# Pooled attention and a squared-ReLU feed-forward: scores as cross products on all rows and the main product on row halves, with a new planned order

## The chip, the cores and the metric

One Trainium2 chip, one core. Times are device microseconds of the whole kernel; the median of three runs before the change is 878.62 us.

## What is computed

```python
def _attn_ref(q, k, v):                       # q, k, v: (4, 8, 1152, 64), float32
    q_pool = q.reshape(B, H, S // 2, 2, D).mean(axis=3)
    scores = (1.0 / np.sqrt(D)) * np.matmul(q_pool, k.transpose(0, 1, 3, 2))
    scores = scores - np.max(scores, axis=-1, keepdims=True)
    attn = np.exp(scores)
    attn = attn / (np.sum(attn, axis=-1, keepdims=True) + 1e-09)
    return np.matmul(attn, v).astype(np.float32)

def _moe_ref(x, w_in, w_out):                 # x: (2304, 512), w_in: (512, 2048), w_out: (2048, 512)
    h = x @ w_in
    r = np.maximum(h, 0.0)
    return ((r * r) @ w_out).astype(np.float32)
```

`reference` puts the heads of `_attn_ref` side by side, 8 x 64 = 512 columns for 4 x 576 rows, and hands them to `_moe_ref`. The feed-forward part works on all rows with one pair of weights.

## The kernel before

Every float32 operand of a product is carried as two float16 parts, a high one (hi) and what is left (lo), and a product is a sum of products of parts in float32. The work falls into **heads in pairs**: 4 batches by 4 pairs are 16 preparations; each pair has nine chunks of 128 queries, 144 chunks in all. Eight of the nine belong to one head (128 queries); the fifth in the list `CH` (its entry is `None`) holds the last 64 queries of both heads. I call the first kind a full and the second a narrow unit.

*Preparation of a pair* (`prep`). k, q and v are loaded (`LK`, `LQ`, `LV`, on the SyncE queue), q is pooled (`QS`), a scale is found, and the parts are written: `KA` writes the hi part of k (a scaled copy, line 315 or 317, on ScalarE or GpSimd), `KD` the lo part (VectorE, line 343, one instruction a head), `KT` transposes both by DMA into a tile `kT` (line 488): its partitions 0 to 63 are the hi part, 64 to 127 the lo part, and its columns the keys in blocks of 128, nine a head. `QA`, `QD`, `QT` do the same for q into `qT[:, 0]`. `QX` (line 509, VectorE or GpSimd) copies the two partition halves of `qT[:, 0]` into `qT[:, 1]` swapped, so that there the lo part is on top. `VA` and `VD` split v.

*A chunk* (`chunk`). `S` makes the scores: for l = 0 (hi on hi plus lo on lo) and l = 1 (lo on hi plus hi on lo) and three stretches of keys (512, 512, 128), a product of all 128 rows into one of two tiles `s` of three PSUM banks (line 572; line 567 for narrow units, whose two heads use one half of the output columns each). `MX` takes the row maximum (VectorE, line 580), `EX` the exponential with its row sum (ScalarE, lines 590 and 591) into a buffer. Then the result is split and transposed: for most chunks `HI` (ScalarE line 595, GpSimd line 340, or VectorE line 599), `LO` (line 603, VectorE or GpSimd) and a DMA transpose `TR` into `PT`; for 28 chunks TensorE transposes (`TP`, line 658) with `TH` and `TL` (lines 667 and 681) copying out. `S` of chunk i waits for `EX` of chunk i - 2.

*A group* (`group`). `PV` (line 723) multiplies the transposed weights with v, two heads at a time on the two halves of the output columns: 54 products of 256 or 320 columns. `ED` copies out.

*Feed-forward blocks* (`block`). Nine blocks of 256 rows: normalise (`RV` to `XR`), scale and split (`XQ` to `XD`), `H` in 8 steps of 24 products of 256 columns (line 865), ReLU and square (`HA` line 875 or 877, `G1` 880, `G2` 885 or 888, `G3` 892), `O` in 8 steps of 12 products of 512 columns (line 914), `OD` and the store. The weights of this part are prepared while attention runs (`WL` to `WD`).

*Order.* Nothing is ordered by hand. `Plan.add` takes each step with its engines and a duration for each in ns, and `Plan.order` builds a list: among the steps that could start soonest, the one with the smallest `prio` goes first, which is its place in the program plus an offset for its kind from `CFG` (`off`, and `off0` before chunk `FB`, behind which the first block could begin). Where a step may run on several engines, the planner picks. The list is issued as it stands: each engine works through its instructions in this order.

Of the kernel before, what the change touches and what calls it, by code (L numbers as in the profile page):

```python
# [56 lines left out]
class Plan:  # L57
# [15 lines left out]
    def add(self, name, engs, deps, emit, at, take=None, give=None, after=()):  # L73

        kind = name[0]
        off, off0 = cfg("off", {}), cfg("off0", {})
        self.at[name] = len(self.ops)
        prio = cfg("nudge", {}).get(len(self.ops), 0.0) + at + off.get(kind, DEF.get(kind, 0.0)) + (off0.get(kind, 0.0) if at < self.early else 0.0)
        self.ops.append(
            dict(name=name, engs=dict(engs), deps=[d for d in deps if d], emit=emit, pos=at, prio=prio, take=take, give=give, after=after)  # L80
        )

    def order(self, last):
# [127 lines left out]
def kernel(  # L211
# [12 lines left out]
    nc = tc.nc  # L224
    B, H, S, D = q.shape
# [7 lines left out]
    KD = DM // 128  # L233
# [63 lines left out]
    add = plan.add  # L297
    tl = {}
# [14 lines left out]
    def scaled(o, out, x, s):  # L313
        if o["eng"] == "ACT":
            nc.scalar.activation(out, x, AF.Copy, scale=s)
        elif o["eng"] == "POOL":
            nc.gpsimd.tensor_scalar(out, x, s, 1.0, op0=ALU.mult, op1=ALU.mult)  # L317
        else:
            nc.vector.tensor_scalar(out, x, s, None, op0=ALU.mult)
# [26 lines left out]
    def prep(n):  # L346
# [39 lines left out]
        def k2():  # L386
            return buf("k2", n).rearrange("p (h c l d) -> p h c l d", h=2, c=9, l=2)
# [89 lines left out]
            add(("GE", n, w), {"POOL": 350}, [("GU", n, w)], lambda o, w=w: ge(o, w), need)  # L477

        def ka(o):
            scaled(o, k2()[:, :, :, 0, :], rk(), tl["psc", n][:, 2, 0:1])  # L480

        def kd(o):
            t, r, s = k2(), rk(), tl["psc", n][:, 2, 0:1]
            for h in range(2):
                split_lo(t[:, h, :, 1, :], r[:, h], s, t[:, h, :, 0, :])

        def kt(o):
            nc.sync.dma_start_transpose(out=kTs[slot], in_=buf("k2", n))
# [51 lines left out]
    def chunk(i):  # L540
# [15 lines left out]
        def scores(o):  # L556
            s = sts[i % 2]
            kt, qt = kTs[slot], qTs[slot]
            for l in range(2):
                for x in range(3):  # L560
                    for h in range(2) if CH[j] is None else CH[j][:1]:
                        st = dict(start=(l == 0), stop=(l == 1), skip_group_check=True)
                        k0, k1 = 4 * x, min(4 * x + 4, 9)
                        rhs = kt[:, h * 9 + k0 : h * 9 + k1, :].rearrange("p a b -> p (a b)")
                        w = 128 * (k1 - k0)
                        if CH[j] is None:
                            nc.tensor.matmul(
                                s[h * 64 : (h + 1) * 64, x, :w], lhsT=qt[:, l, h, 8, :], rhs=rhs, **st
                            )
                        else:  # L570
                            c0 = CH[j][1]
                            nc.tensor.matmul(  # L572
                                s[:, x, :w], lhsT=qt[:, l, h, c0 : c0 + 2, :].rearrange("p a b -> p (a b)"),
                                rhs=rhs, **st
                            )

        def smax(o):
            a = sm_p.tile([128, 2], F32, tag="ca", name="ca", bufs=4)
# [40 lines left out]
        back = []  # L619
        if i >= 2:  # L620
            back = [("TL", i - 2)] if i - 2 in turned and i - 2 not in turned_b else [("EX", i - 2)]
        add(("S", i), {"PE": 1115 if CH[j] is None else 985}, [("KT", n), ("QX", n)] + back, scores, i)
        add(("MX", i), {"DVE": 1275}, [("S", i)], smax, i)
        add(("EX", i), {"ACT": 1500}, [("MX", i), ("GE", n, "qk")] + sold, ex, i, take=(("P", i), ("buf",), cfg("RSV", 1)))

# [77 lines left out]


    GR_ = [0, 1, 1, 0]

    def group(vi, r):
        n, js, i0 = visits[vi]
# [6 lines left out]
        def pv(o):  # L715
            vv = v2s[preps[n]["slot"]]
            px = bank(o)
            tl["px", vi, r] = px
            ps = [(vl, pl, kc) for vl, pl in ((1, 0), (0, 0), (0, 1)) for kc in range(NC)]
            for i, (vl, pl, kc) in enumerate(ps):  # L720
                for h in range(2):
                    t = PTs[gidx[vi, gg[h]] % NPT]
                    nc.tensor.matmul(  # L723
                        px[h * 64 : (h + 1) * 64, :N], lhsT=vv[:, h, kc, vl, :], rhs=t[:, 9 * pl + kc, :N],
                        start=(i == 0), stop=(i == 3 * NC - 1), skip_group_check=True,
                    )

# [466 lines left out]
```

## Time and profile before

| | before |
|---|---|
| median of 3 runs | 878.62 us (876.68 to 881.27) |
| span of the profiled execution | 873.5 us |
| median of the runs less that span | 5.1 us |
| TensorE busy | 743.7 us (85%), 6041 products |
| VectorE busy | 653.3 us (75%) |
| ScalarE busy | 610.7 us (70%) |
| GpSimd busy | 403.0 us (46%) |
| mean granted TensorE clock | 0.946 |

No time of its own is listed for the profiled execution beside its span; the 5.1 us is what the runs' median has above it. Busy times are unions of an engine's instructions, and the ends of products are modelled: what a group of products takes is read from the start of one group to the start of the next, where nothing waits between them. The granted clock is 1.00 at 2.4 GHz and 0.5 at 1.2 GHz; a mean between them is a mix of both. Line numbers are those of the kernel before.

### The profile page before, as it was taken

What the parts mean: (1) busy time and instruction counts of PE and PEld (TensorE: products, weight loads), DVE (VectorE), ACT (ScalarE), POOL (GpSimd) and SP (SyncE); (2) the same over time, 40 slices, a digit from 0 to 9 for tenths busy, and PEclk for the clock granted to TensorE, in tenths of its full rate; (3) what the DMA queues carried; (4) which work ended last, traced back from release to release, by engine and by line L of the source; (5) the groups of instructions that cost most, each with busy time, mean ns of one, the idle gap of its engine ahead of it and who ended that gap; (6) DMA issues with size and microseconds to landing.
All of it is one profiled execution on the core that took longest, in us unless ns stands there. A gap on an engine that the chain in (4) does not pass through costs nothing. (4 is left out here: it accounts for less than half of the span.)

```text
span 873.5 us, 15476 instructions
## 1 busy us (share of the span) xinstructions
PE 743.7 (85%) x6041; PEld 495.6 (57%) x6041; DVE 653.3 (75%) x817; ACT 610.7 (70%) x959; POOL 403.0 (46%) x281
## 2 busy tenths in 40 slices
PE   0567656767579999998999999898999999999997
PEld 0344534544347567754775576566647756858573
DVE  4897999997878887988989788879788974312120
ACT  4666886778988778866896767777767984625150
POOL 2454436755878644555465266537835531100000
PEclk9976877799869999999999999999999999999999
DMA  7798796797668999989998989996889997000001
GB/s 220 223 176 210 163 245 179 184 220 150 134 144 156 174 160 201 164 182 184 173 195 150 197 159 172 204 179 141 153 183 181 183 158 133 2 13 13 13 14 24
DMA packets 346888, 133.39 MB, mean 153 GB/s; under 512 B 330176, under 2 KB 330176, under 8 KB 346816
## 3 DMA queue, kind: packets, MB, share of 16 engines
q1 hardware_dynamic: 346816, 132.41, 74.9%
q8 instruction: 47, 0.77, 0.4%
q14 instruction: 25, 0.20, 0.1%
HBM read 45.09 MB, written 4.72 MB: 57 GB/s over the span
## 5 line engine op out<-in xcount | busy, mean ns | idle before, releaser
L580 DVE TENSOR_REDUCE ca<-s 128x1 f32<-128x1152 f32 x144 | 192.6, 1348 | 13.5 <-PE s L572 8.9
L591 ACT ACTIVATE buf<-s,ca,esc 128x1152 f32<-128x1152 f32 x144 | 188.9, 1312 | 7.7 <-DMA PT<-buf 1.2
L603 POOL TENSOR_TENSOR buf<-buf,buf 128x1152 f16<-128x1152 f32 x60 | 152.6, 2545 | 88.2 <-ACT buf L595 61.9
L865 PEld LDWEIGHTS <-w 128*128 128x128 f16 x1728 | 168.7, 98 | 32.4 <-issue 8.3
L572 PE MATMUL s<-kT,qT 128*128 128x512 f16 (+1 forms) x768 | 156.9, 348 | 18.7 <-ACT buf L591 17.8
L914 PE MATMUL ba<-w,region 128*128 128x512 f16 x624 | 141.6, 379 | 0.7 <-DVE region L797 0.5
L914 PEld LDWEIGHTS <-region 128*128 128x128 f16 x864 | 82.9, 98 | 96.2 <-issue 2.9
L865 PE MATMUL ba<-region,w 128*128 128x256 f16 x1080 | 124.4, 274 | 6.3 <-DVE x L797 3.5
L572 PEld LDWEIGHTS <-qT 128*128 128x128 f16 x768 | 71.9, 105 | 86.1 <-issue 37.5
L723 PE MATMUL ba<-PT,v 128*64 128x256 f16 (+1 forms) x1728 | 116.0, 293 | 5.6 <-DVE PT L681 4.5
L723 PEld LDWEIGHTS <-v 128*64 128x64 f16 x1728 | 97.8, 113 | 22.5 <-issue 12.3
L603 DVE TENSOR_TENSOR buf<-buf,buf 128x1152 f16<-128x1152 f32 x56 | 84.6, 1510 | 14.6 <-ACT buf L595 12.3
L590 ACT ACTIVATE ca<-ca,cols,esc 128x1 f32<-128x1 f32 x144 | 54.6, 379 | 50.4 <-DVE ca L580 49.9
L892 DVE TENSOR_TENSOR region<-region 128x512 f16<-128x512 f32 x41 | 35.0, 854 | 63.0 <-ACT region L885 62.5
L658 PE MATMUL ba<-ident,buf 128*128 128x128 f32 x252 | 47.6, 312 | 35.2 <-DVE PT L681 14.7
L340 POOL TENSOR_SCALAR buf<-buf,cols 128x1152 f16<-128x1152 f32 x31 | 42.6, 1373 | 63.9 <-ACT buf L591 55.9
L595 ACT ACTIVATE buf<-buf 128x1152 f16<-128x1152 f32 x59 | 68.5, 1161 | 2.5 <-DVE buf L603 0.6
L343 DVE SCALAR_TENSOR_TENSOR buf<-raw,psc,buf 128x576 f16<-128x576 f32 x48 | 64.5, 1381 | 5.6 <-POOL buf L317 3.2
L658 PEld LDWEIGHTS ba<-ident,buf 128*128 128x128 f32 x252 | 31.3, 159 | 50.4 <-DVE PT L681 18.9
L892 POOL TENSOR_TENSOR region<-region 128x512 f16<-128x512 f32 x31 | 43.7, 1411 | 32.4 <-ACT region L885 29.5
L667 ACT ACTIVATE PT<-ba 128x384 f16<-128x384 f32 x84 | 39.2, 485 | 20.0 <-PE ba L658 19.4
L914 PE MATMUL bt<-w,region 128*128 128x512 f16 x240 | 52.9, 379 | 0.0
(135 smaller groups left out, 979.7 us busy)
## 6 DMA issues: line engine op xcount, KB each, us to landing
raw<-in_k_dram SPq DMA_DIRECT2D x16, 576.0 KB, 4.6
raw<-in_q_dram SPq DMA_DIRECT2D x32, 288.0 KB, 4.4
raw<-in_v_dram SPq DMA_DIRECT2D x16, 576.0 KB, 4.2
region<-in_moe_w_in_dram SPq DMA_DIRECT2D x8, 1024.0 KB, 5.8
region<-in_moe_w_out_dram SPq DMA_DIRECT2D x8, 1024.0 KB, 5.9
out_dram<-buf SPq DMA_DIRECT2D x36, 128.0 KB, 2.4
PT<-buf SPq DMA_TRANSPOSE x132, 4.8
qT<-buf SPq DMA_TRANSPOSE x32, 3.5
```

Source lines behind the costliest of these rows:

```text
L343: nc.vector.scalar_tensor_tensor(out=o, in0=x, scalar=s, in1=h, op0=ALU.mult, op1=ALU.subtract)
L572: nc.tensor.matmul(s[:, x, :w], lhsT=qt[:, l, h, c0 : c0 + 2, :].rearrange("p a b -> p (a b)"), rhs=rhs, **st)
L580: nc.vector.reduce_max(a[:, 0:1], st3(), axis=AX.X)
L590: nc.scalar.activation(a[:, 1:2], a[:, 0:1], AF.Identity, bias=ln14, scale=tl["esc", n][:, 0:1])
L591: nc.scalar.activation(P(), st3(), AF.Exp, bias=a[:, 1:2], scale=tl["esc", n][:, 2:3], accum_out=col)
L595: nc.scalar.activation(hl()[:, 0], P(), AF.Copy)
L603: e.tensor_tensor(out=hl()[:, 1], in0=P(), in1=hl()[:, 0], op=ALU.subtract)
L658: nc.tensor.matmul(t[:, y], lhsT=P()[:, c * 128 : (c + 1) * 128], rhs=ident, is_transpose=True, start=(y == 0), stop=False, skip_group_che ...
L723: nc.tensor.matmul(px[h * 64 : (h + 1) * 64, :N], lhsT=vv[:, h, kc, vl, :], rhs=t[:, 9 * pl + kc, :N], start=(i == 0), stop=(i == 3 * NC - ...
L865: nc.tensor.matmul(ph[:, f2], lhsT=w16[0][:, SLOT[f // 4], wl, a, f % 4 * 128 : (f % 4 + 1) * 128], rhs=xhl()[:, xl, a], start=(i == 0), s ...
L892: e.tensor_tensor(out=gt[u][:, 1], in0=rt[u % 2], in1=gt[u][:, 0], op=ALU.subtract)
L914: nc.tensor.matmul(p[:, :DM], lhsT=g[:, gl, f % 2, tt * 128 : (tt + 1) * 128], rhs=w16[1][:, SLOT[f // 4], wl, f % 4], start=(f == 0 and g ...
```

## The change

Three things. **Scores:** a unit no longer has the product lo on lo. The cross products (lo on hi plus hi on lo) still run on all rows, and hi on hi runs on one half of the rows: the upper half from `qT[:, 0]`, the lower half from `qT[:, 1]`. For that every second key block of the first eight is stored in `kT` with its parts swapped, lo on top. The output is in the order of `KO`, and `PV` reads the value blocks in that order. **Preparation:** `KA` and `KD` write the even and the odd blocks apart, so each of their instructions becomes two. **Order:** all numbers of `CFG` are new; a table `COST` replaces the planner's durations of sixteen pairs of step and engine, and the price of `S` goes from 985 to 790 ns (1115 to 900 for narrow units).

```diff
-CFG = {'SPLIT': 0, ... 'pen': 863.62, 'bl': 3.86, 'slPE': 172.93, 'slACT': 71.23, 'slDVE': 99.26, ...
+CFG = {'SPLIT': 0, ... 'pen': 990.252, 'bl': 22.1123, 'slPE': 94.4706, 'slACT': 9.4041, 'slDVE': 112.8356, ...
...
+COST = {
+    ("EX", "ACT"): 1710, ("RV", "DVE"): 1800, ("WS3", "DVE"): 1010, ("WS1", "DVE"): 456, ("HI", "ACT"): 1070,
+    ("HI", "POOL"): 1190, ("KA", "POOL"): 1500, ("VA", "POOL"): 1190, ("XU", "POOL"): 1250, ("KA", "ACT"): 1330,
+    ("VA", "ACT"): 1160, ("QA", "ACT"): 666, ("HA", "ACT"): 625, ("G1", "ACT"): 655, ("QX", "POOL"): 3000, ("QX", "DVE"): 980,
+}
...
+        engs = {e: COST.get((kind, e), c) for e, c in engs.items()}
...
         def ka(o):
-            scaled(o, k2()[:, :, :, 0, :], rk(), tl["psc", n][:, 2, 0:1])
+            for z in range(2):
+                scaled(o, k2()[:, :, z::2, z, :], rk()[:, :, z::2], tl["psc", n][:, 2, 0:1])
 
         def kd(o):
             t, r, s = k2(), rk(), tl["psc", n][:, 2, 0:1]
             for h in range(2):
-                split_lo(t[:, h, :, 1, :], r[:, h], s, t[:, h, :, 0, :])
+                for z in range(2):
+                    split_lo(t[:, h, z::2, 1 - z, :], r[:, h, z::2], s, t[:, h, z::2, z, :])
...
-            for l in range(2):
-                for x in range(3):
-                    for h in range(2) if CH[j] is None else CH[j][:1]:
...
+            if CH[j] is None:
+                hs = [(h, slice(h * 64, h * 64 + 64), slice(8, 9)) for h in range(2)]
+            else:
+                hs = [(CH[j][0], slice(0, 128), slice(CH[j][1], CH[j][1] + 2))]
+
+            def mm(rows, l, x, start):
+                for h, po, cs in hs:
+                    ks = slice(h * 9 + 8, h * 9 + 9) if x == 2 else slice(h * 9 + x, h * 9 + 8, 2)
+                    w = 128 if x == 2 else 512
+                    nc.tensor.matmul(
+                        s[po, x, :w].rearrange("p (a b) -> p a b", b=128),
+                        lhsT=qt[rows, l, h, cs, :].rearrange("p a b -> p (a b)"), rhs=kt[rows, ks, :],
+                        start=start, stop=not start, skip_group_check=True,
+                    )
+
+            every, up, dn = slice(0, 128), slice(0, 64), slice(64, 128)
+            mm(every, 1, 0, True)
+            mm(every, 1, 2, True)
+            mm(every, 0, 1, True)
+            mm(up, 0, 0, False)
+            mm(dn, 1, 1, False)
+            mm(up, 0, 2, False)
...
-        add(("S", i), {"PE": 1115 if CH[j] is None else 985}, [("KT", n), ("QX", n)] + back, scores, i)
+        add(("S", i), {"PE": 900 if CH[j] is None else 790}, [("KT", n), ("QX", n)] + back, scores, i)
...
+    KO = [0, 2, 4, 6, 1, 3, 5, 7, 8]
...
-                        px[h * 64 : (h + 1) * 64, :N], lhsT=vv[:, h, kc, vl, :], rhs=t[:, 9 * pl + kc, :N],
+                        px[h * 64 : (h + 1) * 64, :N], lhsT=vv[:, h, KO[kc], vl, :], rhs=t[:, 9 * pl + kc, :N],
```

What the new order moves, at three places, all on VectorE. The names: `psc` holds a pair's scales, `raw` its loaded data, `buf` work buffers, `w_0` and `w_1` the feed-forward weights, `ba` a PSUM bank, `s` the scores, `x` and `region` block data, `xs` a block's scale, `ca` row maxima. In the changed file the same lines stand 8 to 16 further on (line 343 is 351, 580 is 595, 509 is 519).

The parts of the first pair, before:

```order
L457 RECIPROCAL psc<-psc 128x2
L343 SCALAR_TENSOR_TENSOR buf_94<-raw_101,psc,buf_94 128x9x64
L343 SCALAR_TENSOR_TENSOR buf_93<-raw_100,psc,buf_93 128x9x64 x2
L982 TENSOR_SCALAR w_0_90<-w_0_90 128x1024
L986 SCALAR_TENSOR_TENSOR w_0_90<-region,w_0_90 128x1024
```

and now:

```order
L465 RECIPROCAL psc<-psc 128x2
L351 SCALAR_TENSOR_TENSOR buf_94<-raw_101,psc,buf_94 128x9x64
L351 SCALAR_TENSOR_TENSOR buf_93<-raw_100,psc,buf_93 128x5x64
L351 SCALAR_TENSOR_TENSOR buf_93<-raw_100,psc,buf_93 128x4x64
L351 SCALAR_TENSOR_TENSOR buf_93<-raw_100,psc,buf_93 128x5x64
L351 SCALAR_TENSOR_TENSOR buf_93<-raw_100,psc,buf_93 128x4x64
L998 TENSOR_SCALAR w_0_90<-w_0_90 128x1024
```

The two instructions on k's lo part are four, of five and four blocks.

A little later in the same pair, before the first scores, VectorE before:

```order
L440 TENSOR_SCALAR psc<-ba_116 128x1
L444 TENSOR_SCALAR psc<-psc 128x1
L451 TENSOR_SCALAR psc<-psc 128x1
L457 RECIPROCAL psc<-psc 128x1
L343 SCALAR_TENSOR_TENSOR v_0_106<-raw_101,psc,v_0_106 128x9x64 x2
```

and now:

```order
L448 TENSOR_SCALAR psc<-ba_116 128x1
L519 COPY qT_104<-qT_104 64x1152 x2
L452 TENSOR_SCALAR psc<-psc 128x1
L459 TENSOR_SCALAR psc<-psc 128x1
L465 RECIPROCAL psc<-psc 128x1
```

The swap copies of q stood on GpSimd and now stand here; of 32 such copies VectorE has 30 and had 16.

Around the first feed-forward operand (the `xs` row on `x_111`), before:

```order
L599 CAST buf_94<-buf_95 128x1152
L343 SCALAR_TENSOR_TENSOR buf_93<-x_111,xs,buf_93 128x1024
L343 SCALAR_TENSOR_TENSOR region<-region,xs 128x1024
L580 TENSOR_REDUCE ca<-s_113 128x1
L580 TENSOR_REDUCE ca<-s_114 128x1
L877 TENSOR_SCALAR region<-ba_116 128x512
```

and now:

```order
L465 RECIPROCAL psc<-psc 128x1
L351 SCALAR_TENSOR_TENSOR buf_99<-x_111,xs,buf_99 128x1024
L595 TENSOR_REDUCE ca<-s_114 128x1
L351 SCALAR_TENSOR_TENSOR v_1_107<-raw_101,psc,v_1_107 128x9x64 x2
L595 TENSOR_REDUCE ca<-s_113 128x1
L839 TENSOR_SCALAR ba_116,xs<-ba_116 128x256
```

44 row maxima stood ahead of this operand and 39 stand ahead of it now. On TensorE 46 score units stood ahead of the first `H` product and 41 do now, so 98 and 103 lie between it and the end of the scores; behind the last scores stand 576 `H` and 336 `O` products in both.

## Rows read from the trace of the kernel before

**Rows 1.** Three stages: length, busy us of each engine (instructions), clock, DMA share, GB/s.

```profile
0.00:259.70 259.70, 154.86 (x1251) 102.09 (x1251) 219.75 (x295) 197.55 (x284) 147.60 (x95) 0.84 0.79 188
259.70:720.50 460.80, 441.15 (x3689) 295.46 (x3687) 393.62 (x457) 354.82 (x584) 248.55 (x176) 0.99 0.93 173
720.50:873.50 153.00, 147.72 (x1106) 98.06 (x1103) 39.88 (x67) 58.34 (x92) 6.83 (x12) 0.99 0.16 30
```

**Rows 2.** TensorE in order of time, 268 to 284 us: start, us, instructions.

```profile
268.55 1.14 PE L572 MATMUL s<-kT,qT 128*128 128x512 f16 x6
269.53 2.78 PE L865 MATMUL ba<-buf,w 128*128 128x256 f16 x24
272.15 1.14 PE L572 MATMUL s<-kT,qT 128*128 128x512 f16 x6
```

**Rows 3.** The same view, 436 to 460 us.

```profile
444.88 1.14 PE L572 MATMUL s<-kT,qT 128*128 128x512 f16 x6
445.95 3.86 PE L723 MATMUL ba<-PT,v 128*64 128x320 f16 x54
449.74 1.15 PE L572 MATMUL s<-kT,qT 128*128 128x512 f16 x6
...
455.17 1.17 PE L567 MATMUL s<-kT,qT 128*64 128x512 f16 x12
456.26 0.88 PE L658 MATMUL ba<-ident,buf 128*128 128x128 f32 x6
```

**Rows 4.** The same view, 718 to 750 us (L785 uses 32 rows, 64 columns).

```profile
722.02 3.14 PE L723 MATMUL ba<-PT,v 128*64 128x256 f16 x54 [0.38 <-DVE PT L681]
725.09 2.76 PE L914 MATMUL ba<-w,region 128*128 128x512 f16 x12
727.78 0.63 PE L785 MATMUL bt<-ru,pick 32*64 32x128 f16 x16
```

**Rows 5.** The chain that ended last, in order of time, its longest piece.

```profile
848.21 20.73 PE bt L914 x96
```

**Rows 6.** TensorE in order of time, 240 to 262 us.

```profile
244.76 2.13 PE L572 MATMUL s<-kT,qT 128*128 128x512 f16 x6
...
252.31 4.00 PE L572 MATMUL s<-kT,qT 128*128 128x512 f16 x12 [4.30 <-ACT buf L591]
```

**Rows 7.** Single lines' instructions: duration ns min/median/max, first and last start us.

```profile
L580 DVE TENSOR_REDUCE ca<-s x144: 1332/1347/1359, 26.4 to 722.3; 128x1 f32<-128x1152 f32 x144
L343 DVE SCALAR_TENSOR_TENSOR buf<-raw,psc,buf x48: 802/817/4151, 12.9 to 681.4; 128x576 f16<-128x576 f32 x48
L343 DVE SCALAR_TENSOR_TENSOR region<-region,xs x5: 1274/1285/3125, 257.1 to 766.6; 128x1024 f16<-128x1024 f32 x5
L509 POOL COPY qT<-qT x16: 1141/1481/2182, 19.1 to 691.5; 64x1152 f16<-64x1152 f16 x16
L509 DVE COPY qT<-qT x16: 453/455/2539, 56.9 to 647.9; 64x1152 f16<-64x1152 f16 x16
L603 DVE TENSOR_TENSOR buf<-buf,buf x56: 1340/1359/2497, 89.3 to 727.7; 128x1152 f16<-128x1152 f32 x56
L888 DVE TENSOR_TENSOR region<-region x4: 680/1506/2861, 518.7 to 666.0; 128x512 f32<-128x512 f32 x4
```

**Rows 8.** Stretches of 25 us, columns as in rows 1.

```profile
0.00:25.00 25.00, 4.08 (x24) 3.09 (x25) 11.65 (x25) 11.15 (x13) 7.71 (x13) 1.00 0.82 239
...
425.00:450.00 25.00, 23.61 (x219) 18.12 (x215) 22.34 (x27) 22.09 (x37) 19.72 (x14) 1.00 1.04 180
450.00:475.00 25.00, 24.15 (x193) 15.56 (x192) 24.34 (x28) 18.83 (x33) 14.88 (x11) 1.00 0.82 161
```

**Rows 9.** TensorE's longest wait, 259.7 to 720.5 us: total, times, longest.

```profile
PE ba L865 <- DVE x L797: 3.5, 1, 3.5
```

**Rows 10.** Weight loads of the scores, full and narrow: ns min/median/max.

```profile
L572 PEld LDWEIGHTS <-qT x768: 95/98/292, 23.7 to 721.2; 128*128 128x128 f16 x192
L567 PEld LDWEIGHTS <-qT x192: 106/110/178, 47.4 to 715.5; 128*64 128x64 f16 x192
```

More of the change, by code (lines that the diff above doesn't have):

```diff
@@ new lines @@
+CFG = {'SPLIT': 0, 'TURN': [], 'TURNB': [0, 2, 4, 6, 8, 10, 12, 14, 16, 18, 20, 22, 24, 26, 28, 30, 32, 34, 40, 49, 58, 67, 76, 85, 94, 103, 112, 121, 130, 139], 'WDP': ((1, 0), (1, 1), (1, 2), (1, 3)), 'WSP': 1.1964, 'WOF': 2.9814, 'MSP': 11.3411, 'pen': 990.252, 'bl': 22.1123, 'slPE': 94.4706, 'slACT': 9.4041, 'slDVE': 112.8356, 'slPOOL': 358.7205, 'slSP': 9.5752, 'off': {'ED': -0.89, 'EX': 1297.61, 'G1': -124.17, 'G2': -71.47, 'G3': -536.72, 'GE': -3151.39, 'GF': -725.99, 'GM': -8.92, 'GR': -683.97, 'GS': -1595.84, 'GT': -6452.08, 'GU': -2406.64, 'GW': -3701.11, 'H': 1008.55, 'HA': -36.07, 'HI': 2217.4, 'KA': 3343.01, 'KD': -6.85, 'KT': -611.08, 'LK': -8.08, 'LO': -0.89, 'LQ': -1155.12, 'LV': -3849.84, 'MX': -2.6, 'O': 1009.69, 'OD': -1813.97, 'PV': 967.92, 'QA': 4826.65, 'QD': -869.17, 'QK': -3548.84, 'QQ': -299.99, 'QS': -995.17, 'QT': -1620.04, 'QV': -1290.22, 'QX': -2243.97, 'RB': -870.78, 'RT': -28.55, 'RU': 93.56, 'RV': 341.33, 'S': -37.64, 'ST': 1497.38, 'TH': -175.63, 'TL': -238.81, 'TP': -35.69, 'TR': 2.53, 'VA': 15.77, 'VD': -1467.0, 'W1': 55.93, 'W2': 125.39, 'W3': -45.53, 'W4': 167.8, 'W5': 1.22, 'WA': 37.34, 'WB': 7.21, 'WD': 613.14, 'WG': -144.34, 'WL': -14.51, 'WM': 1449.49, 'WS1': -414.49, 'WS2': 469.86, 'WS3': -2.1, 'XA': 3980.46, 'XD': 3.02, 'XM': 2286.4, 'XN': 683.65, 'XQ': -2825.2, 'XR': -498.09, 'XT': 1536.26, 'XU': -295.85, 'XW': -565.22}, 'off0': {'ED': 127.27, 'EX': 140.98, 'G2': -39.2, 'G3': -76.82, 'GE': -0.18, 'GF': 48.34, 'GM': -0.07, 'GR': -98.03, 'GS': -1671.27, 'GT': -295.88, 'GU': -470.84, 'GW': -27.74, 'H': -140.16, 'HA': 410.09, 'HI': 2.93, 'KA': 15.85, 'KD': -1974.42, 'KT': -316.15, 'LK': 1.3, 'LO': 281.97, 'LQ': -53.72, 'LV': 35.17, 'O': -457.25, 'PV': 53.38, 'QA': 341.53, 'QD': 0.0, 'QK': 86.58, 'QQ': -225.91, 'QS': 506.03, 'QT': -310.09, 'QV': 8.34, 'QX': 54.45, 'RB': -1.42, 'RT': 285.45, 'RU': -145.72, 'RV': 0.36, 'S': -78.72, 'TH': 805.26, 'TL': -1906.67, 'TP': -83.92, 'TR': 3.79, 'VA': 406.73, 'VD': -35.68, 'W1': 219.78, 'W2': 260.31, 'W3': 42.01, 'W4': 250.33, 'WA': -351.58, 'WB': 270.75, 'WD': -3039.68, 'WG': 48.48, 'WL': -900.11, 'WM': -2830.86, 'WS1': 956.01, 'WS2': -1010.0, 'WS3': 93.01, 'XA': -352.61, 'XD': -55.34, 'XN': 319.37, 'XQ': 8.42, 'XR': 29.39, 'XT': -261.36, 'XU': -6.49, 'XW': -187.26}}
@@ L78, in add @@
         prio = cfg("nudge", {}).get(len(self.ops), 0.0) + at + off.get(kind, DEF.get(kind, 0.0)) + (off0.get(kind, 0.0) if at < self.early else 0.0)
+        engs = {e: COST.get((kind, e), c) for e, c in engs.items()}
         self.ops.append(
-            dict(name=name, engs=dict(engs), deps=[d for d in deps if d], emit=emit, pos=at, prio=prio, take=take, give=give, after=after)
+            dict(name=name, engs=engs, deps=[d for d in deps if d], emit=emit, pos=at, prio=prio, take=take, give=give, after=after)
         )
@@ L558, in scores @@
             kt, qt = kTs[slot], qTs[slot]
-            for l in range(2):
-                for x in range(3):
-                    for h in range(2) if CH[j] is None else CH[j][:1]:
[L562 to L575, printed above, removed]
+            if CH[j] is None:
[18 more added lines that the diff above has]
+            mm(up, 0, 2, False)
         def smax(o):
```

1 line of the change is left out of this document (removed).

## The prediction

> **What bounds the kernel now.** I read the three stages first [rows 1]. They are cut where TensorE starts its first feed-forward product (259.7 us) and where it starts its last scores (720.5 us). In the first stage TensorE is busy 154.9 of 259.7 us at a mean granted clock of 0.84, and VectorE 219.8 us, 84.6%. In the middle stage TensorE is busy 441.2 of 460.8 us, so it idles 19.7 us, while VectorE has 393.6 us (85.4%) and ScalarE 354.8 us (77%). In the tail TensorE has 147.7 of 153.0 us and the others little. So the first stage belongs to VectorE and the chains around it, the middle stage to TensorE with VectorE not far behind, and the tail to TensorE alone. The chain that ended last says the same of the tail: its longest piece is 96 products of 512 columns [rows 5].
>
> Next I read what one score unit costs, from start to start, since ends are modelled. A full unit that begins at 268.55 is followed by the next work at 269.53, so it takes 0.98 us; the 24 products of 256 columns behind it take 2.62 us [rows 2]. That is 6,144 columns in 2.62 us, 0.426 ns a column, and 2,304 score columns at that rate are 0.98 us: both granted clocks are 1.00 there, and no weight load shows. In the first stage TensorE is not what the stage waits for: a full unit there lasted 2.13 us where it lasts 1.14 us later (both with the modelled end), the clock being at its lower level for it, and yet the next score unit in that view first waited 4.30 us for ScalarE [rows 6].
>
> **The change part by part.** *The score unit.* Six passes of 512, 512, 128, 512, 512 and 128 columns become 512, 128 and 512 columns on all rows, two passes of 512 on one row half each, and one of 128 on a half. If the two halves run together, 1,792 columns are left, 0.764 us; 0.218 us goes. That halves of the array can run together is shown for column halves: 54 products of 320 columns take 3.79 us from start to start [rows 3], where one after the other they would need 54 x 320 x 0.426 ns = 7.4 us.
>
> What the trace of before lacks is a product that uses 64 rows and all 128 columns. Its nearest rows are the changes of array form that are there. A score unit in front of column-half products takes 1.07 us and not 0.98 [rows 3]: 0.09 us to go in. Twelve products of 512 columns are 20.73 / 8 = 2.59 us [rows 5], and 2.69 us in front of products on 32 rows by 64 columns [rows 4]: 0.10 us. Coming out costs as much at most: 27 pairs of 320 columns are 3.68 us and took 3.79 us. The narrow unit (two heads by 64 queries, column halves) takes 1.09 us [rows 3], that is 0.11 us above the full one. The Trainium skill, "TensorEngine Tiling (Array Packing)", section Key Properties, says that a change of tiling mode drains TensorE; by that rule each new unit would pay going in and coming out, and most of the 0.218 us would be gone. The trace agrees for the forms it has, by the 0.09 to 0.11 us above.
>
> So a full unit will cost between 0.764 us (no cost of the form) and 0.96 us (0.10 us each way). Both forms that show the cost have weights 64 columns wide, and their weight load takes 110 ns where one of 128 columns takes 98 [rows 10]; the new form keeps 128 columns. The planner's own price of a full unit, 985 ns before, equals the 0.98 us of the trace; the change writes 790. For these two reasons I take 0.80 us for the full unit and 0.90 for the narrow one, near the lower end, and keep 0.96 and 0.97 for a rival.
>
> *VectorE's added work.* The low parts of k are written by four instructions per head pair and not two. 576 elements take 817 ns, 1,024 take 1,285 [rows 7]: 1.045 ns an element and 0.215 us fixed, so 0.43 us a head pair. The swap copies of q move to VectorE: 30 of 32 stand there now, 16 before; 0.455 us each, against 1.481 us on GpSimd [rows 7].
>
> *First stage.* In the new order VectorE's first feed-forward operand stands behind 39 row maxima and not 44, with the same weight preparation before it. Counted up to there: five maxima of 1.347 us less (-6.7), twelve more k pieces (+2.6), eight more swap copies (+3.6), one 128x1152 subtraction less (-1.4), the rest about 0: -2 us of VectorE [rows 7]. ScalarE and TensorE each lose five score chains. I take -4 us for the stage. The bounds: with VectorE as dense as the trace has it elsewhere, some 89% over this stage without its first 25 us (11.7 of them busy [rows 8]), the stage would be 218 / 0.887 = 246 us, -14; with its new pieces waiting on one another, +5.
>
> *Middle stage.* It now holds 103 score units (91 full, 12 narrow) and not 98 (87 and 11), one more attention-value group (54 products, 3.07 to 3.79 us, I take 3.4 [rows 3, 4]) and six more transposes (0.9 us [rows 3]); the feed-forward products in it are the same 1,152 and 528. Scores were 87 x 0.98 + 11 x 1.09 = 97.3 us and are 91 x 0.80 + 12 x 0.90 = 83.6 us. TensorE: -13.7 + 3.4 + 0.9 = -9.4 us. It idled 19.7 us only, and its longest wait there was 3.5 us [rows 9], so I take the whole 9.4 us as time. The cover to watch is VectorE: five more maxima (+6.7), 20 more pieces of k (+4.3), six more swap copies (+2.7), seven more squares on it, at 0.68 us each if none waits (+4.8), three subtractions less (-4.1), the rest +1: 393.6 becomes 409 us in a stage of 451, 90.7%. The first stage without its start held 89%, and two stretches of 25 us stand at 22.34 and 24.34 us [rows 8], so I hold that to be possible.
>
> *Tail.* The same 576 and 336 products stand behind the last scores: 0. Nothing of the tail is covered, so it keeps its 153 us.
>
> *Key order.* Value blocks are read in another order, as many and as large: 0, whatever hides it. GpSimd gives up 14 swap copies (-20.7 us) and takes other work; it is busy 248.6 of 460.8 us and has room [rows 1]. The transfers are as many as before; their engines' share is 0.93 in the middle stage [rows 1], and the same work in 9 us less makes that 0.95.
>
> Sum: -4 - 9.4 + 0 = -13.4 us; 873.5 becomes 860.1 us of span. The median of the runs, 878.62, lies 5.1 us above the profiled span, so I forecast 865 us. About 0.5%, 4.4 us, is what a measurement here can tell from no change: 874.2 to 883.0 us counts as the same.
>
> **The rivals.**
>
> 1. *The forms cost what they cost elsewhere.* Then a full unit is 0.98 - 0.218 + 0.20 = 0.96 us, a narrow one 0.97. Middle scores: 91 x 0.96 + 12 x 0.97 = 99.0 us, +1.7; with the group and the transposes +6.0. With -4 from the first stage: +2, 881 us. For it: three places with 0.09 to 0.11 us each. Against it: all three are forms with 64 columns. Chance 0.25.
>
> 2. *VectorE becomes the bound, and the kernel gets slower.* It works through a fixed order, and 409 us at the share it had in the middle stage, 85.4%, need 479 us, +18; with -4 it is +14, 893 us. The point from which it decides: below a share of 88% the middle stage is over 465 us and the 4 us of the first stage are gone. For it: the work moves onto VectorE, and some squares there took far over their 0.68 us, median 1.5 us [rows 7]. Against it: much of its idle time was TensorE's doing, in a stage where TensorE was full. Chance 0.12.
>
> 3. *The row halves do not run together.* The change then does not do what it is built for: a full unit costs 0.98 us and the 0.20 us of the forms, a narrow one 1.29; 91 x 1.18 + 12 x 1.29 = 122.9 us, +25.6, with the group and the transposes +29.9, with -4 it is 905 us. Against it: the column pairs above. Chance 0.04.
>
> 4. *The new order packs better than I count.* First stage -14, units at 0.764 and 0.87 us (80.0 us in the middle, -17.3 + 4.3 = -13): -27, 852 us. For it: the prices of sixteen operations are replaced, and VectorE is idle 40 us in the first stage. Against it: VectorE would need over 91% of the middle stage. Chance 0.14.
>
> **How the numbers follow.** The forecast has the other 0.45; its own spread, by the first stage's +5 and -14 and units of 0.764 to 0.86 us, is 852 to 874 us. Faster by over 0.5%: 0.44 of the forecast, 0.14 of rival 4 and 0.05 of rival 1, 0.63. Same: 0.01, 0.13 of rival 1 and 0.02 of rival 2, 0.16. Slower: 0.07 of rival 1, 0.10 of rival 2 and 0.04 of rival 3, 0.21. For 8 in 10 the range must take in rival 1 and the nearer part of rivals 2 and 4: 847 to 889 us.
>
> **What would show it.** Start to start, a full score unit in front of a full product at clock 1.00: 0.80 us is the forecast, 0.96 rival 1, 1.18 rival 3. The first feed-forward product begins near 256 us, the last scores near 707 us. VectorE's share of the middle stage near 91% with TensorE idle about 20 us is the forecast; TensorE idle 35 us or more, waiting on buffers that VectorE empties, is rival 2. I am wrong if the unit falls to 0.80 us and the middle stage does not shrink, or if the first stage moves by more than 14 us either way.

## The result, and the profile after

The changed kernel takes 885.13 us (median of 4 runs, 884.06 to 887.93), the kernel before 877.65 us beside it: 1.0086 times as long, interval 1.0058 to 1.0114. It is 7.5 us slower; 865 us was forecast, so the direction was wrong. The profiled execution has a span of 882.9 us, 9.4 us above that of before.

The three stages after, cut at the same two events as [rows 1], same columns:

```profile
0.00:252.67 252.67, 156.55 (x1152) 100.61 (x1153) 216.23 (x307) 182.48 (x260) 123.50 (x79) 0.75 0.78 182
252.67:730.05 477.38, 452.18 (x3783) 288.26 (x3782) 409.44 (x498) 365.66 (x606) 265.75 (x188) 0.97 0.93 173
730.05:882.90 152.85, 147.93 (x1109) 98.01 (x1106) 39.68 (x68) 55.16 (x88) 12.45 (x15) 1.00 0.16 30
```

The first stage is 7.0 us shorter, the middle stage 16.6 us longer (460.8 to 477.4), the tail the same. In the middle stage VectorE has 409.4 us of work, what was counted (409), but TensorE has 452.2 us where the forecast had some 432, and idles 25.2 us, not 19.7.

TensorE in order of time, around 265 to 276 us, then around 715 us (compare [rows 2] and [rows 3]):

```profile
264.69 1.02 PE L578 MATMUL s<-kT,qT 128*128 128x512 f16 x6 [1.09 <-ACT buf L606]
265.66 3.14 PE L739 MATMUL ba<-PT,v 128*64 128x256 f16 x54
268.73 1.04 PE L578 MATMUL s<-kT,qT 128*128 128x512 f16 x6
269.70 2.79 PE L881 MATMUL ba<-buf,w 128*128 128x256 f16 x24
272.33 1.03 PE L578 MATMUL s<-kT,qT 128*128 128x512 f16 x6
273.29 2.79 PE L881 MATMUL ba<-buf,w 128*128 128x256 f16 x24
...
715.25 1.99 PE L578 MATMUL s<-kT,qT 128*128 128x512 f16 x12
717.18 3.86 PE L739 MATMUL ba<-PT,v 128*64 128x320 f16 x54
```

A full unit takes 0.96 us from start to start (272.33 to 273.29), two in a row 1.93. It was 0.98. So the 512 columns that went brought 0.02 us, not 0.18. Where the rest is, the unit at 272.33 shows in stretches of 10 ns, score products alone (length, busy us, then the three columns clock, DMA share and GB/s); the number in brackets is how many were in flight, pipeline ends included:

```profile
272.59:272.60 0.01, 0.01 (x2) 1.00 0.66 154
272.60:272.61 0.01, 0.01 (x3) 1.00 1.11 179
...
272.90:272.91 0.01, 0.01 (x1) 1.00 0.06 0
272.91:272.92 0.01, 0.01 (x3) 1.00 0.00 0
...
273.13:273.14 0.01, 0.01 (x2) 1.00 0.00 0
273.14:273.15 0.01, 0.01 (x3) 1.00 0.00 0
```

The third all-row pass begins at 272.60 and has 0.218 us of columns, to 272.82. The two row halves begin together in one stretch of 10 ns, but at 272.91: 0.09 us in which no pass begins and none has columns left. They take 0.23 us together, the last pass begins at 273.14 and has 0.055 us of columns, and the next work begins at 273.29: another 0.095 us. The halves do run side by side, and going into the form and out of it eats what that saves.

The weight loads around this unit (PEld is TensorE's loading of weights):

```profile
272.22 0.42 PEld L578 LDWEIGHTS <-qT 128*128 128x128 f16 x3
272.91 0.11 PEld L578 LDWEIGHTS <-qT 64*128 64x128 f16 x3 [0.26 <-issue]
273.29 0.33 PEld L881 LDWEIGHTS <-w 128*128 128x128 f16 x4 [0.26 <-issue]
```

The unit's first weights, behind work of the same form, begin to load 0.11 us before its first pass. Behind each change of form the first load is recorded only where the pass itself begins, after 0.26 us without a load. One load takes 0.098 us [rows 10], about as long as each gap; whether the gap is that load, no longer made ahead, or something else in the change of form, no run separates.

VectorE's instructions of two lines (ns min/median/max; compare [rows 7]); the pieces of k's lo part are there, and 30 swap copies:

```profile
L351 DVE SCALAR_TENSOR_TENSOR buf<-raw,psc,buf x80: 472/543/3006, 12.9 to 685.2; 128x320 f16<-128x320 f32 x32, 128x256 f16<-128x256 f32 x32, 128x576 f16<-128x576 f32 x16
L519 DVE COPY qT<-qT x30: 453/456/2532, 21.9 to 693.6; 64x1152 f16<-64x1152 f16 x30
```

### The profile page after: what moved, and what is told of

Same layout as the page of the kernel before. It is cut to its first block, busy times and chain, and to the rows that moved or that the text cites. A ratio compares the mean times of both kernels' runs of the same rounds, so it can differ in the third digit from the quotient of the medians.

```text
span 882.9 us, 15522 instructions
## 1 busy us (share of the span) xinstructions
PE 756.7 (86%) x6041; PEld 486.9 (55%) x6041; DVE 665.3 (75%) x871; ACT 603.3 (68%) x953; POOL 401.7 (45%) x281
## 5 line engine op out<-in xcount | busy, mean ns | idle before, releaser
L618 POOL TENSOR_TENSOR buf<-buf,buf 128x1152 f16<-128x1152 f32 x65 | 165.5, 2548 | 83.4 <-ACT buf L610 50.7
L578 PE MATMUL s<-kT,qT 128*128 128x512 f16 (+3 forms) x960 | 164.9, 357 | 9.8 <-ACT buf L606 7.7
L881 PE MATMUL ba<-region,w 128*128 128x256 f16 x1128 | 133.8, 278 | 1.3 <-DVE region L351 0.6
L739 PE MATMUL ba<-PT,v 128*64 128x256 f16 (+1 forms) x1728 | 125.0, 307 | 8.9 <-DVE PT L696 5.1
L739 PEld LDWEIGHTS <-v 128*64 128x64 f16 x1728 | 106.5, 119 | 25.9 <-issue 15.2
L578 PEld LDWEIGHTS <-qT 128*128 128x128 f16 (+3 forms) x960 | 57.6, 103 | 95.3 <-issue 73.9
L673 PE MATMUL ba<-ident,buf 128*128 128x128 f32 x252 | 52.8, 337 | 49.8 <-DVE PT L696 34.8
L618 DVE TENSOR_TENSOR buf<-buf,buf 128x1152 f16<-128x1152 f32 x51 | 77.1, 1514 | 11.0 <-ACT buf L610 5.4
L908 DVE TENSOR_TENSOR region<-region 128x512 f16<-128x512 f32 x37 | 30.2, 815 | 55.9 <-ACT region L901 52.2
L351 DVE SCALAR_TENSOR_TENSOR buf<-raw,psc,buf 128x256 f16<-128x256 f32 (+2 forms) x80 | 62.2, 829 | 1.4 <-POOL buf L325 1.4
```

Source lines behind the costliest of these rows:

```text
L351: nc.vector.scalar_tensor_tensor(out=o, in0=x, scalar=s, in1=h, op0=ALU.mult, op1=ALU.subtract)
L578: nc.tensor.matmul(s[po, x, :w].rearrange("p (a b) -> p a b", b=128), lhsT=qt[rows, l, h, cs, :].rearrange("p a b -> p (a b)"), rhs=kt[row ...
L618: e.tensor_tensor(out=hl()[:, 1], in0=P(), in1=hl()[:, 0], op=ALU.subtract)
L673: nc.tensor.matmul(t[:, y], lhsT=P()[:, c * 128 : (c + 1) * 128], rhs=ident, is_transpose=True, start=(y == 0), stop=False, skip_group_che ...
L739: nc.tensor.matmul(px[h * 64 : (h + 1) * 64, :N], lhsT=vv[:, h, KO[kc], vl, :], rhs=t[:, 9 * pl + kc, :N], start=(i == 0), stop=(i == 3 * ...
L881: nc.tensor.matmul(ph[:, f2], lhsT=w16[0][:, SLOT[f // 4], wl, a, f % 4 * 128 : (f % 4 + 1) * 128], rhs=xhl()[:, xl, a], start=(i == 0), s ...
```

## The experiments

All ratios are to the kernel before, timed on the same chip in the same rounds; differences in us are the ratio's difference times 877. "Old order" is the order of the kernel before, instruction by instruction, "new order" that of the changed one.

**1. The scores alone, in the old order.** The edit: the change's `ka`, `kd`, `scores` and `KO`, without its `CFG`, `COST` and price of `S`.

> The new scores and the new way of writing k, in the old order (old CFG, old prices of the planner). Form theory (a change of array form costs some 0.1 us each way, so a full unit still takes 0.96 us): start to start 0.96 us in place of 0.98, TensorE gains 2 us in the middle stage, VectorE pays 7 us more for the pieces of k and is not the bound: 876 to 880 us, within 0.5% of before. VectorE theory (the loss of the change is VectorE's added work): 882 us or more.

882.26 us, ratio 1.0052 (1.0029 to 1.0075): 4.6 us slower. Its first two stages:

```profile
0.00:264.33 264.33, 164.09 (x1252) 98.28 (x1252) 220.53 (x307) 198.17 (x288) 146.36 (x96) 0.76 0.78 185
264.33:728.54 464.21, 439.07 (x3689) 280.66 (x3687) 401.47 (x477) 356.15 (x590) 246.68 (x181) 0.99 0.91 172
```

In the middle stage TensorE has the 2 us less work that were expected (439.1 after 441.2), and the stage is 3.4 us longer all the same.

**2. The order alone.** The edit: the change's `CFG`, `COST` and price of `S`, without the rest.

> The old scores and the old way of writing k, in the new order (new CFG, COST and the price of 790 for a unit that takes 980). Form theory: the loss sits in the order, which was planned with a unit 0.17 us too cheap, so this is as slow as the changed kernel, 883 to 888 us. VectorE theory: 7 us of VectorE's work is gone, so it comes back to 876 to 880 us.

879.07 us, ratio 1.0020 (0.9998 to 1.0043): no clear difference, 1.8 us. Its first two stages:

```profile
0.00:250.15 250.15, 152.90 (x1153) 103.90 (x1154) 212.24 (x295) 182.01 (x256) 123.83 (x77) 0.81 0.78 184
250.15:726.70 476.55, 454.26 (x3783) 304.67 (x3782) 406.37 (x478) 364.35 (x599) 265.61 (x185) 0.98 0.94 174
```

The new order ends the first stage 9.6 us sooner and pays it back in the middle stage, which got five score units and one attention-value group more and is 15.8 us longer, with the old scores. So the loss of the change is not the order's, at least not most of it; but the longer middle stage is.

Such differences of stages come from one execution each. The profiled one of the kernel before was fast for its kernel: all its later runs lie 2.2 to 2.3 us above their own spans, which puts it near 875.7 us where the median is 877.65. Stage differences to [rows 1] therefore add up to some 2 us too much, and the profiled executions of the other versions lie up to 4 us off their medians.

**3. Two more changes of form, and none.** In the new order, with everything else as in the change. First:

```diff
             mm(every, 1, 2, True)
+            mm(up, 0, 2, False)
             mm(every, 0, 1, True)
             mm(up, 0, 0, False)
             mm(dn, 1, 1, False)
-            mm(up, 0, 2, False)
...
```

> The changed kernel with the last half-row pass moved ahead of the third all-row pass: the same passes, the same columns, but four changes of array form a unit and not two. Form theory: 0.19 us more a unit, a full unit 1.15 us, +20 us in the middle stage and a little in the first: 903 to 912 us. Rival (the two gaps of 0.095 us belong to the first half-row weight load or to the end of a unit, not to the form): a unit stays at 0.96 us and the time at 885 us.

903.90 us, ratio 1.0304 (1.0262 to 1.0346): 19 us above the change, for the same columns. TensorE in order of time:

```profile
274.94 1.24 PE L578 MATMUL s<-kT,qT 128*128 128x512 f16 x6
276.11 2.79 PE L881 MATMUL ba<-buf,w 128*128 128x256 f16 x24
```

A unit takes 1.17 us, 0.21 more than 0.96. So the gaps belong to the change of form, with whatever comes with it (each change also brings a weight load that is not made ahead). Then none:

```diff
-            mm(up, 0, 0, False)
-            mm(dn, 1, 1, False)
-            mm(up, 0, 2, False)
+            mm(every, 0, 0, False)
+            mm(every, 0, 2, False)
```

> The changed kernel with the half-row passes replaced by one all-row pass of 512 and one of 128 columns: 1,792 columns a unit as intended, no change of form. Left out: the hi on hi product of the odd key blocks (its output is not the scores). Form theory: a full unit takes 0.77 us, 0.19 us less for 103 units of the middle stage, -20 us: 863 to 868 us, which is also what the forecast stood for. VectorE theory (VectorE bounds the middle stage with its 409 us): 880 us or more, TensorE idling longer.

872.64 us, ratio 0.9947 (0.9926 to 0.9968): 12 us below the change, where 20 were expected. The form theory carries the larger part; something else keeps 8 us. TensorE in order of time, and the first stage:

```profile
270.33 0.92 PE L578 MATMUL s<-kT,qT 128*128 128x512 f16 x5
271.09 2.78 PE L880 MATMUL ba<-buf,w 128*128 128x256 f16 x24
```

```profile
0.00:251.90 251.90, 151.19 (x1107) 105.95 (x1108) 216.46 (x307) 182.38 (x260) 124.51 (x79) 0.75 0.79 183
```

A unit without change of form takes the 0.76 us of its columns.

**4. The pieces of k alone and the row halves alone, in the old order.** Pieces: the two loops over `z` of `ka` and `kd`, writing to the old places. Halves: the change's `scores` and `KO` without these loops.

> The kernel before with k's parts written in pieces (four lo instructions a pair in place of two, two hi in place of one), at the old places, with the old scores and the old order. VectorE theory (the 0.5% that the new scores lost in the old order is the 7 us of pieces, of which the stages that VectorE shares in pay the larger part): +3 to +5 us, 880 to 882 us. Clock theory (the loss is the lower granted clock of the first stage, 0.76 where it was 0.84, which the half-row passes bring): 0 to +1 us, 877 to 878 us.

882.31 us, ratio 1.0063 (1.0040 to 1.0087): 5.5 us, the whole loss of experiment 1.

> The new scores in the old order with k's parts written as before. Left out: the swapped storing of the odd key blocks, so their scores are not the reference's. VectorE theory: no added VectorE work, 875 to 877 us, a full unit still 0.96 us. Clock theory: the first stage is 3 to 5 us longer than before at a lower granted clock, 880 to 882 us.

878.20 us, ratio 1.0018 (1.0005 to 1.0031): 1.6 us. The first two stages, of the pieces and then of the halves:

```profile
0.00:262.76 262.76, 159.40 (x1252) 104.70 (x1252) 222.38 (x307) 198.25 (x288) 147.41 (x97) 0.81 0.78 186
262.76:726.91 464.15, 442.81 (x3689) 296.40 (x3688) 399.49 (x477) 356.12 (x590) 248.03 (x180) 0.99 0.93 172
```

```profile
0.00:261.46 261.46, 162.86 (x1251) 97.94 (x1251) 217.39 (x295) 197.72 (x284) 146.64 (x94) 0.76 0.78 187
261.46:724.16 462.70, 438.69 (x3689) 280.54 (x3688) 393.46 (x457) 354.63 (x584) 251.06 (x177) 0.99 0.93 173
```

With the pieces the first stage is 3.1 us longer than in [rows 1] and the middle stage 3.4, and VectorE is busy 2.6 and 5.9 us more in them. TensorE was taken for the bound of the middle stage, at 441 of 461 us, and yet more than half of what VectorE got there arrived at the end. With the halves the first stage is 1.8 us longer, at a granted clock of 0.76 and not 0.84, and the middle stage 1.9 us, though TensorE has 2.5 us less work in it. So the VectorE theory has the larger part. That the lower clock makes the 1.8 us is not shown.

**5. Which pieces.** Only the hi part in two pieces (`ka`), the lo part as before, old order.

> The kernel before with only the hi part of k written in two pieces (ScalarE or GpSimd), the lo part as before, old scores and old order. If the 5.5 us that the pieces cost are VectorE's four lo instructions, this is 876 to 878 us; if the longer way from the scale to the lo part (ScalarE or GpSimd first) costs as much, 879 us or more.

878.12 us, ratio 0.9996 (0.9978 to 1.0015): nothing. It is the lo part, four instructions of VectorE in place of two.

**6. Neither forms nor pieces, in the new order.** Experiment 3 without forms, `ka` and `kd` as before.

> The version without change of form (1,792 columns a unit, no half rows) and with k's parts written as before, in the new order. Left out: the hi on hi product of the odd key blocks and their swapped storing. If VectorE with its 413 us is what kept the 20 us of TensorE's relief from arriving (12 did), 7 us less of its work bring 4 to 7 us: 866 to 869 us, the forecast's 865 nearly. If TensorE's lower clock and its waits in the fixed order keep them, 0 to 2 us: 871 to 873 us.

866.14 us, ratio 0.9872 (0.9851 to 0.9894): 6.6 us below the version with pieces. Its first two stages:

```profile
0.00:248.87 248.87, 148.45 (x1108) 104.63 (x1109) 210.41 (x295) 181.90 (x256) 125.16 (x77) 0.77 0.81 185
248.87:707.86 458.99, 432.58 (x3670) 295.04 (x3668) 405.52 (x478) 363.08 (x599) 268.75 (x185) 0.98 0.96 180
```

This is nearly the forecast's kernel, without the pieces (its units take 0.76 us, the forecast had 0.80), and it runs at the forecast's time: TensorE has the 432 us that were forecast. But the time is not made up as forecast: the first stage is 10.8 us shorter and not 4, the middle stage 1.8 us and not 9.4, with 26.4 us of idle TensorE.

**7. Sharing the change of form between two units.** In the new order, where two units follow each other on TensorE (25 places), the all-row passes of both come first and the half-row passes of both behind.

```diff
...
+            late.append(halves)
+            if not o["pair"]:
+                while late:
+                    late.pop(0)()
...
```

> The changed kernel where two neighbouring units (25 places, 15 of them in the middle stage) make their all-row passes first and their half-row passes behind, so that the two share one change of form each way. Form theory: 0.19 us less a pair, -3 us in the middle stage and up to -1.5 in the first: 880 to 882 us, and 1.73 us for two units where they took 1.92. Rival: the first unit of a pair is ready 0.5 us later for VectorE, which eats it: 885 us or more.

888.30 us, ratio 1.0124 (1.0103 to 1.0145): 3.3 us worse than the change. TensorE in order of time, and its longest wait of the first stage (total, times, longest):

```profile
706.21 0.65 PE L579 MATMUL s<-kT,qT 128*128 128x512 f16 x3
707.19 1.29 PE L579 MATMUL s<-kT,qT 128*128 128x512 f16 x9 [0.33 <-ACT buf L613]
...
718.85 1.78 PE L579 MATMUL s<-kT,qT 128*128 128x512 f16 x12
720.56 3.86 PE L746 MATMUL ba<-PT,v 128*64 128x320 f16 x54
```

```profile
PE ba L680 <- DVE PT L703: 34.3, 14, 5.7
```

Two units take 1.71 us where they took 1.93, as the form theory has it. But the first of the two is ready later: at 707.19 the second one waits 0.33 us for ScalarE, and the first one's half-row passes stand behind it. The middle stage won 0.9 us only, and the first stage became 4.3 us longer (it ends at 256.97). That the later scores made it so is argued and not shown: the wait of 34.3 us was 31.2 us in the change already.

**8. Other orders.** The kernel before with `COST`, a score unit priced at what it takes (985, 1115), and offsets found anew against the planner's own end time, once from those of the change, once from those of before.

> The kernel before (old scores, old way of writing k) with a third order: the changed kernel's planner durations (COST), but a score unit priced at what it takes (985 and 1115), and the offsets found anew, starting from the changed kernel's. If an order planned with true prices can do better than the first two, 864 to 872 us; if an order changes as little as the second did, 875 to 880 us.

887.20 us, ratio 1.0104 (1.0076 to 1.0131).

> As the third order, but the offsets were found starting from those of the kernel before: 864 to 872 us if true prices help, 875 to 880 us if they do not.

879.89 us, ratio 1.0024 (1.0006 to 1.0042). True prices of the scores did not make an order that is better on the chip, and one of the two is slower than either expectation. Then the new scores and the pieces in the third order:

> The new scores and the pieces of k in the third order. If what they cost does not hang on the order (5.5 us for the pieces, 1 to 2 us for the half-row passes), this is 6 to 8 us slower than the third order with the old scores.

900.65 us, ratio 1.0257 (1.0226 to 1.0288): 13 us above the third order with the old scores, not 6 to 8. What the scores cost hangs on the order; why it is double there was not followed up.

**9. The lo part with as many instructions as before, and with fewer.** If blocks are counted over both heads, every second one swapped, two lo instructions a pair are enough for the new scores:

```diff
...
-            for h in range(2):
-                for z in range(2):
-                    split_lo(t[:, h, z::2, 1 - z, :], r[:, h, z::2], s, t[:, h, z::2, z, :])
+            kk, rr = t.rearrange("p h c l d -> p (h c) l d"), r.rearrange("p h c d -> p (h c) d")
+            for z in range(2):
+                split_lo(kk[:, z::2, 1 - z, :], rr[:, z::2], s, kk[:, z::2, z, :])
...
```

(`ka` is written in the same way, and `scores` and `KO` follow: the second head's even blocks are the swapped ones.) In the change's own order:

> The changed kernel, complete and in its own order, with the swapped blocks counted over both heads, so that the lo part of k needs two instructions a pair and not four. Fixed-time theory: 5 to 6 us less than the changed kernel's 885, 879 to 880 us, and what is left of its loss is 2 to 3 us of half-row passes and order. Otherwise 884 us or more.

879.33 us, ratio 1.0037 (1.0022 to 1.0052): 4.3 us off the change's loss, somewhat less than expected. In the old order:

> The new scores, complete, in the old order with two lo instructions a pair: as the half-row passes alone, 877 to 880 us. If the pieces' cost came from elsewhere, 881 us or more, as the scores alone with four.

877.08 us, ratio 0.9995 (0.9980 to 1.0011): the new scores, complete, are as fast as the old ones. Experiment 1 steps over every second block just as this run does and differs in the number of instructions, so it is the number and not the step that cost 5 us. The 1.6 us of the halves alone do not show in this run. And with the lo part of v in one instruction a pair as well:

> As the run before, and the lo part of v by one instruction a pair: 16 instructions of VectorE less than the kernel before. Fixed-time theory: 2 to 3 us less than with two for v, 875 to 877 us; a little below the kernel before or level with it.

874.75 us, ratio 0.9981 (0.9964 to 0.9998): 1.7 us below the kernel before. Last, the other way round, the kernel before with old scores and one lo instruction a pair for k and one for v:

```diff
-            for h in range(2):
-                split_lo(t[:, h, :, 1, :], r[:, h], s, t[:, h, :, 0, :])
+            split_lo(t[:, :, :, 1, :], r, s, t[:, :, :, 0, :])
...
```

> The kernel before with the lo parts of k and of v written by one instruction a pair each, not two: 32 instructions of VectorE less, old scores, old order. If the fixed 0.215 us of an instruction is what counts, 6.9 us of VectorE's work are gone and, as the pieces cost 5.5 us for 6.9, 4 to 6 us come back: 871 to 874 us, faster than both kernels. If it is the shape of the work or if the longer instructions keep others waiting, 876 to 879 us.

872.26 us, ratio 0.9951 (0.9927 to 0.9974): 4.3 us below the kernel before, and the fastest of all versions that compute everything. Its instructions (ns min/median/max):

```profile
L343 DVE SCALAR_TENSOR_TENSOR buf<-raw,psc,buf x32: 803/1410/4743, 13.3 to 677.3; 128x576 f16<-128x576 f32 x16, 128x1152 f16<-128x1152 f32 x16
L343 DVE SCALAR_TENSOR_TENSOR v<-raw,psc,v x16: 1410/1427/4178, 24.6 to 692.3; 128x1152 f16<-128x1152 f32 x16
```

Of the second line, 1,427 ns for 1,152 elements stand against twice 817 for 576 [rows 7]: 0.21 us saved for each instruction that goes, the fixed time of the prediction. By it 32 instructions are 7 us of VectorE's work; without them the kernel is 4.3 us faster, with 32 more 5.5 us slower. So the number of lo instructions is the cause of what the pieces cost.

That they act by their fixed time alone is not shown. VectorE's whole busy time is 637.0 us here, 653.3 in the kernel before and 661.8 with the pieces, but 645.3 in experiment 5, which changed none of its instructions. So a single profile moves by 8 us without a cause in the code and cannot confirm the 7. And some lo instructions take far longer than the shortest: those of [rows 7] had a median of 817 ns and a mean of 1,381 (the number behind the group's busy us):

```profile
L343 DVE SCALAR_TENSOR_TENSOR buf<-raw,psc,buf 128x576 f16<-128x576 f32 x48 | 64.5, 1381 | 5.6 <-POOL buf L317 3.2
```

What lengthens them was not looked into.

## Why the prediction was wrong, point by point

The change is 20 us above the forecast. Without the changes of form it comes down by 12 us (experiment 3), without k's pieces by another 6.6 (experiment 6), and that is 1 us above the forecast.

- **The score unit: the step that failed first.** I took 0.80 us for it, near the lower end, because the forms that show a cost in the kernel before have weights 64 columns wide and because the planner's new price was 790. It is 0.96 us, the upper end and rival 1 to the hundredth: the row half with 128 columns pays 0.09 us in and 0.095 us out, much as the column halves do. The rule of the Trainium skill, "TensorEngine Tiling (Array Packing)", section Key Properties, that a change of tiling mode drains TensorE, agrees with these gaps. Of their inside the runs show only that no weight load is made ahead across them. The three nearest rows all said 0.09 to 0.11 us, and I set them aside for a difference of which no row showed that it matters. With 0.96 us and the rest of my working, rival 1 gave 881 us.
- **VectorE's added work: near in size, wrong as covered.** The middle stage has the 409 us that were counted, and the fixed time of 0.215 us is met; in the pieces alone VectorE was busy 8.5 us more where I counted 7. I let all of the middle stage's added work lie beside TensorE's, since VectorE was at 85% there. The pieces alone cost 5.5 us. A share of 85% in a fixed order is no cover: in the middle stage 3.4 of 5.9 us came through.
- **First stage, -4 us:** -7.0, inside my bounds. The order alone had -9.6. My bound of -14 spread the 89% over the first 25 us too, where only 11.65 us are busy; with these kept apart the same density gives -2. In the run VectorE had 216.2 us of work and was busy 89.6% behind the first 25 us.
- **Middle stage, -9.4 us:** +16.6. The new order has +15.8 with the old scores; the 0.18 us a unit that I took off there did not come, 18 us over the stage's units. Rival 1's working has +6.0 of the 16.6. The rest shows as 5 us of TensorE's busy time beyond that, at a mean granted clock of 0.97 where it was 0.99, and 5.5 us of idle time. Of the 5 us, 2.35 stand at the start of the stage, where 24 products of 256 columns took 4.97 us and not 2.62, at the lower clock level nearly throughout (with the old scores in this order 5.06 us):

```profile
252.67:257.64 4.97, 4.97 (x25) 3.48 (x24) 4.96 (x7) 4.32 (x6) 0.34 (x1) 0.52 1.07 256
```

- **Tail, 0:** 152.9 us after 153.0, right.
- **From span to time, 5.1 us:** too much. In the change a run lies 1.8 us above its span, in the kernel before 2.2 to 2.3; the other 3 us were this one fast profile against the median of three.
- **The sum as such:** without the forms and the pieces 866 us were measured where it gives 865, and a good part of that is luck: -10.8 and -1.8 us of the two stages stand where it has -4 and -9.4 (in an execution of 862.5 us).
- **Rival 2** named VectorE with a deciding share of 88%. The share stayed at 85.8%, so its point was passed, but at 885 us and not at 893, and TensorE idled 25 us and not 35. It was a part of the truth beside rival 1. **Rival 3** fell: the halves run together. **Rival 4** fell as a whole, though its sign for the first stage was right: neither this order nor the two others made the kernel before faster.

By the parts measured one by one the loss of 7.5 us closes: 5.5 us for the lo pieces, 0 to 1.6 for the half-row passes (experiments 9 and 4), 1.8 for the order make 7.3 to 8.9, each with an interval of 1 to 2 us to either side. In the change's own order the pieces are worth 4.3 us (experiment 9), and in the third order scores and pieces together 13 (experiment 8), so the parts add up only roughly and not in every order.

## What to carry to other kernels

Before splitting a product over halves of the array, count the changes of form: here each pair of them cost as much as some 450 columns at the full clock, so a split that saves 512 columns and comes alone between other forms saves next to nothing. An engine that was busy 85% in a fixed order was not idle enough here to hide work on it: count its instructions, and merge those whose elements can be addressed together, which gave 0.5% here for two lines. And a forecast that meets the time has to be checked stage by stage. A planner's own price for a new instruction is a claim to be measured first, and a better plan by its own reckoning need not be better on the chip.

## What the runs showed of the hardware beyond what was expected

The granted clock of the first stage, a mean over its two levels, is lower wherever a score unit has fewer columns, with row halves and without. In the old order it is 0.84 with the old scores [rows 1], 0.81 with the old scores and k's pieces, and 0.76 with the new scores (experiments 1 and 4). In the new order it is 0.81 with the old scores (experiment 2), 0.75 in the change, and 0.75 and 0.77 in the two versions that have 1,792 columns a unit and no half-row pass (experiments 3 and 6). So the half rows as such do not make it. In the middle stage it is 0.97 to 0.99 in all of these. What the clock answers to was not tried.
